# A fused attention and expert kernel on one core: queries' exponentials as weights, division with tokens on partitions

## The chip, the core and the metric

The kernel runs on one core of a Trainium2 chip. The metric is the device time of one execution in microseconds (us). Three runs of the kernel before took 1261.27 to 1263.55 us, median 1263.35 us.

## What is computed

Three parts follow each other. First a linear attention with 4 batches, 8 heads, 576 tokens and 64 features a head:

```python
def phi(x):
    proj = np.einsum('bhsd,df->bhsf', x, w_phi)
    proj = proj - np.max(np.abs(proj), axis=-1, keepdims=True)
    return np.concatenate([np.exp(proj), np.exp(-proj)], axis=-1)
q_p, k_p = (phi(q), phi(k))
kv = np.einsum('bhsf,bhsd->bhfd', k_p, v)
num = np.einsum('bhsf,bhfd->bhsd', q_p, kv)
den = np.einsum('bhsf,bhf->bhs', q_p, np.sum(k_p, axis=2))[..., None] + 1e-06
return num / den
```

Its output, 2304 tokens of width 512, goes through four experts, weighted by the rows' shares `p`: `out += p[:, e:e+1] * (relu(x @ w1[e]) @ w2[e])`, with an inner width of 1024. Last comes `((x @ v1) * (x @ v2) @ w3) @ w_out`. All data are fp32.

## The kernel before, in words

Two heads of one batch make a pair; there are 16 pairs, `p` from 0 to 15. For each pair, `k_side(p)` (L506) projects the keys (tile `P`, L540), takes each token's largest absolute value, subtracts it, forms the two exponentials (`E`, L525) and sums the products with the values, to which columns of ones are appended, into `kvp` (L553). Projections of the two heads stand on different halves of the rows of TensorE's array, the sums on different halves of its columns ("tiled" below). The result goes to `KV`.

`q_side(p, KV)` (L605) treats each head's 576 queries in two slices of 288 tokens, with the features on partitions. The host has written each q twice, and L613 and L614 make of the copies a rounded part and a remainder, stacked on 128 partitions. Two matmuls (L623, L624) project them, ScalarE copies the result (L628), GpSimd takes the largest absolute value over the partitions (L631), VectorE subtracts it (L634), and ScalarE forms the exponentials `Eq` (L639). The product with `KV` (L655) gives numerators on 64 partitions and the denominator, repeated, on the other 64. For pairs 6 to 15 (`SPLIT`), `KV` and `Eq` are split into rounded part and remainder (L594, L645, L647) and multiplied in three passes; for pairs 0 to 5 the product is in fp32. In the records an fp32 matmul counts as two instructions. ScalarE copies the product to `xq` (L660). One row of denominators a head is gathered by DMA to `d9` (L664), inverted (L667, L670), written to DRAM (L671) and read back to all partitions (L675); VectorE multiplies (L680) into the rows `xr`. These DMAs are all issued by SP. `plain_x` splits the first blocks of tokens for the experts.

The experts' work is a list of visits (L745). A visit holds a quarter of an expert's inner width and one or more blocks of 384 tokens (`pairs` there are pairs of blocks). In the plain form (`plain_up`, L806) a block has 24 up matmuls of 384 columns; in the Strassen form (`strassen_up`, L812) two blocks have 42. A block's `down` (L863) has three groups of six matmuls of 512 columns, each summed by VectorE (L890). The first `KA` = 8 quarters are plain for the first two blocks, so that they can run between the parts of attention; for the first `EB` = 5 of them each block has a visit of its own. When all attention is done, `phase_c` (L1053) closes the pools of attention, and the Strassen visits begin. The folds (L930) multiply `w3` and `w_out` into one matrix, two before each of the first `KA` visits of the second round.

No engine's order is written by hand. Every operation is given to `Prog` with an engine, an estimated time and a priority; `simulate` (L148) places it when its inputs are there and a buffer of its tile is free, `deadlines` (L254) gives the other engines due times from TensorE's order, and the order found is what is issued. Each engine then works in order. Up to `FILLED` (110 us of the planned time) `run` (L281) puts matmuls on zeros (`filler`, L472, tile `fill_z`) where the plan leaves TensorE idle. `AHEAD` (L62) says where in the visits the pairs from 4 on are due. PSUM has eight banks: in attention three for the visits (`mma`) and five for attention (`kv` 1, `kp` 2, `qp` 1, `num` 1).

## Time and profile before

| | before |
|---|---|
| median of 3 runs | 1263.35 us |
| the profiled execution | 1263.01 us |
| its span in the trace | 1261.2 us |
| TensorE busy | 1247.6 us, 99% |
| VectorE busy | 934.2 us, 74% |
| ScalarE busy | 628.4 us, 50% |
| GpSimd busy | 546.9 us, 43% |

In the rows PE is TensorE (PEld its weight loads), DVE VectorE, ACT ScalarE, POOL GpSimd, SP SyncE, which issues the DMAs. A timeline row is a run of equal instructions: start and length in us, engine, line, operation, output<-inputs, shapes, count, and in brackets idle time before it and what ended it. Matmuls overlap in the array, so a run's length includes the way through it; the next run's start shows when it has left the entrance free. The span is from the first to the last record; the profiled execution's own time has 1.8 us more.

### The profile page before, as it was taken

The page shows a single profiled execution, that of the slowest core. Times are in us where ns is not written, and L with a number is a line of the kernel's source. Part 1 is how long each engine was busy: PE and PEld are TensorE (multiplying, and loading weights), DVE is VectorE, ACT ScalarE, POOL GpSimd, SP SyncE. Part 2 cuts the span into 40 slices and gives each one's busy share as a digit, 9 for nine tenths or more (in the row PEclk, how much of TensorE's full clock was granted, in tenths as well). Part 3 has the DMA queues.
Part 4 walks back from the last instruction along what each step waited for, and adds up shares of the span by engine and source line. Part 5 has one row for each costly group of instructions (what it writes and reads, how often), then busy time and mean ns, then how long its engine had stood idle before and what let it go on. Part 6 is the DMA issues. An engine that isn't in the chain of part 4 may idle for free.

```text
span 1261.2 us, 19437 instructions
## 1 busy us (share of the span) xinstructions
PE 1247.6 (99%) x7449; PEld 1125.8 (89%) x7449; DVE 934.2 (74%) x1446; ACT 628.4 (50%) x1231; POOL 546.9 (43%) x374
## 2 busy tenths in 40 slices
PE   8999999999999999999999999999999999999998
PEld 7779988899999999988889888898899999999997
DVE  6698999979787885587687785698998647634454
ACT  7888888745433333344434343454445545443321
POOL 3432323316333333054544455466676677435220
PEclk9999999999999999999999999999999999999999
DMA  5654454222333321023535432143332212211002
GB/s 173 176 183 130 146 176 140 79 88 84 109 110 109 109 92 43 19 87 121 163 121 176 145 131 83 52 134 115 123 100 78 79 51 84 84 34 51 1 1 100
DMA packets 53197, 128.55 MB, mean 102 GB/s; under 512 B 10352, under 2 KB 14832, under 8 KB 53104
## 3 DMA queue, kind: packets, MB, share of 16 engines
q1 hardware_dynamic: 53104, 127.32, 31.5%
q8 instruction: 58, 0.95, 0.3%
q14 instruction: 35, 0.29, 0.1%
HBM read 109.84 MB, written 17.38 MB: 101 GB/s over the span
## 4 chain that ended last, share of the span: by engine, by line
PE 90%; DVE 5%; DMA 2%; ACT 2%; issue 1%; SPq 0%; DVEq 0%; ACTq 0%
PE dn L869 38%; PE upa L800 13%; PE upb L800 7%; PE up L800 4%; PE psw L940 3%; PE upc L800 3%; PE num L655 3%; PE kvp L553 1%; PE upa_4a L800 1%; PE upa_3b L800 1%; PE upa_3a L800 1%; PE upa_5b L800 1%; PE upa_5a L800 1%; PE upa_4b L800 1%; DVE xr L680 1%
## 5 line engine op out<-in xcount | busy, mean ns | idle before, releaser
L869 PE MATMUL dn<-w_b,h 128*128 128x512 f32 x1728 | 423.7, 391 | 0.0
L869 PEld LDWEIGHTS dn<-w_b,h 128*128 128x128 f32 x1728 | 320.7, 188 | 57.5 <-DVE acc L890 0.3
L391 POOL TENSOR_TENSOR w_a<-raw_a,w_a 128x768 fp32r<-128x768 f32 (+2 forms) x80 | 165.5, 2069 | 227.5 <-ACT w_a L389 202.1
L890 DVE SCALAR_TENSOR_TENSOR acc<-dn,pn,acc 128x512 f32<-128x512 f32 x270 | 200.3, 745 | 54.5 <-PE dn L869 52.6
L391 POOL TENSOR_TENSOR w_b<-raw_b,w_b 128x1024 fp32r<-128x1024 f32 x48 | 122.7, 2555 | 228.3 <-ACT w_b L389 223.2
L631 POOL PARTITION_ALL_REDUCE M<-Ps x64 | 86.4, 1361 | 169.5 <-ACT Ps L628 135.0
L800 PE MATMUL upa<-x_T,w_a 128*128 128x384 f32 x720 | 146.2, 337 | 0.0
L800 PEld LDWEIGHTS upa<-x_T,w_a 128*128 128x128 f32 x720 | 128.5, 187 | 7.2 <-ACT s L823 0.7
L823 ACT COPY s<-upa 128x384 f32<-128x384 f32 x120 | 57.5, 479 | 121.2 <-PE upa L800 120.9
L419 POOL TENSOR_TENSOR raw_a<-raw_a 128x256 f32<-128x256 f32 x128 | 109.8, 858 | 18.3 <-DVE acc L890 6.2
L389 ACT CAST w_b<-raw_b 128x1024 fp32r<-128x1024 f32 x61 | 64.3, 1054 | 103.4 <-PE dn L869 62.7
L869 PE MATMUL dn<-w_b,g 128*128 128x512 f32 x432 | 105.7, 390 | 0.0
L389 ACT CAST w_a<-raw_a 128x1024 fp32r<-128x1024 f32 (+2 forms) x93 | 84.5, 908 | 41.1 <-PE upb L800 16.6
L869 PEld LDWEIGHTS dn<-w_b,g 128*128 128x128 f32 x432 | 80.5, 188 | 13.7
L800 PE MATMUL up<-x_B,w_a 128*128 128x384 f32 x384 | 72.2, 338 | 0.0
L655 PE MATMUL num<-Eq,KV 128*128 128x288 f32 x336 | 67.4, 334 | 3.3 <-ACT xq L660 1.8
L800 PEld LDWEIGHTS up<-x_B,w_a 128*128 128x128 f32 x384 | 66.2, 188 | 1.0
L655 PEld LDWEIGHTS num<-Eq,KV 128*128 128x128 f32 x336 | 51.8, 188 | 10.9 <-ACT xq L660 3.8
L639 ACT ACTIVATE Eq<-Ps 128x288 f32<-128x288 f32 x128 | 51.5, 458 | 15.7 <-DVE Ps L634 15.4
L920 DVE TENSOR_TENSOR oacc<-dn,oacc 128x512 f32<-128x512 f32 x54 | 36.8, 687 | 19.0 <-PE dn L869 18.8
L800 PE MATMUL upa<-x_B,w_a 128*128 128x384 f32 x240 | 49.1, 339 | 0.0
L800 PE MATMUL upb<-x_B,w_a 128*128 128x384 f32 x240 | 49.0, 339 | 0.0
(213 smaller groups left out, 2241.7 us busy)
## 6 DMA issues: line engine op xcount, KB each, us to landing
raw_a<-w SPq DMA_DIRECT2D x37, 512.0 KB, 3.4
raw_b<-w SPq DMA_DIRECT2D x37, 512.0 KB, 3.7
qr<-qT SPq DMA_DIRECT2D x32, 288.0 KB, 3.2
near<-w3T SPq DMA_DIRECT2D x16, 512.0 KB, 4.2
raw_b<-near_wo SPq DMA_DIRECT2D x16, 512.0 KB, 4.3
near<-v SPq DMA_DIRECT2D x16, 512.0 KB, 4.8
vx<-vt SPq DMA_DIRECT2D x16, 330.0 KB, 4.3
kr<-kT SPq DMA_DIRECT2D x15, 320.0 KB, 3.9
```

What stands on the lines that cost most here:

```text
L389: lambda: op(ACT, act(n, sbuf), lambda: nc.scalar.copy(out=hi(), in_=raw[1]()), reads=[*raw[:1], *raw[2:]], fills=[w], after=after),
L391: lambda: op(eng, ns, lambda: e.tensor_tensor(out=lo(), in0=raw[1](), in1=hi().bitcast(F32), op=ALU.subtract), reads=[raw[0], w, *raw[2:]] ...
L419: ops.append(lambda to=to, a=a, b=b, how=how: op(POOL, gp(256), lambda: nc.gpsimd.tensor_tensor(out=raw()[:, to], in0=raw()[:, a], in1=raw ...
L631: op(POOL, 1300, lambda M=M, Ps=Ps: nc.gpsimd.partition_all_reduce(M(), Ps(), channels=128, reduce_op=bass_isa.ReduceOp.absmax), reads=[Ps ...
L639: op(ACT, act(HS), lambda a=a, E=E, Ps=Ps: nc.scalar.activation(out=E()[:, a], in_=Ps(), func=AF.Exp, scale=1.0 - 2 * a), reads=[Ps], fill ...
L655: nc.tensor.matmul(num(), KV[i]()[:, a, 2 * h:2 * h + 2].rearrange("p c d -> p (c d)"), EE[j]()[:, a], start=n == 0, stop=n == len(parts) - 1)
L800: nc.tensor.matmul(ps(), w()[:, a, i, kk * 128:kk * 128 + 128], x()[:, j, kk], start=first and n == 0, stop=last and n == total - 1, skip_ ...
L823: op(ACT, act(TB, False), lambda: nc.scalar.copy(out=t(), in_=ps()), reads=[ps], writes=[t], after=start["C"])
L869: nc.tensor.matmul(ps(), hs[fc]()[:, x, t * 128:(t + 1) * 128], w()[:, fc * 2:fc * 2 + 2, y], start=fc == 0 and n == 0, stop=fc == 1 and n ...
L890: op(DVE, dve(DM) + 61, lambda a=a, ps=ps, share=share: nc.vector.scalar_tensor_tensor(out=a(), in0=ps(), scalar=share(), in1=a(), op0=ALU ...
L920: op(DVE, dve(DM), lambda a=a, ps=ps: nc.vector.tensor_tensor(out=a(), in0=ps(), in1=a(), op=ALU.add), reads=[ps], writes=[a])
L940: nc.tensor.matmul(ps(), wa[v]()[:, k, a, f * 128:f * 128 + 128], wb[v]()[:, 2 * k:2 * k + 2, b], start=g == 0 and k == 0 and n == 0, stop ...
```

## The change

**Queries.** q comes once, with the two heads on the two halves of the partitions. A pair's 576 tokens are two chunks of 256 and 320; for pairs 0 to 3 a chunk of 384 comes first and the other 192 tokens after pair 3's first chunk (`BACK`). Rounded part and remainder of q are projected in three passes, each head on 64 rows of the array, the heads alternating; pair 0 in fp32. The exponentials are now the weights: 64 tokens at a time, on one half of the array's columns, with 66 columns of `KV` moving, in fp32 for every pair. Numerators and denominator come out with tokens on partitions; VectorE adds 1e-6, takes the reciprocal and multiplies, TensorE turns each tile of 128 tokens back (`turn`), and ScalarE copies it to `xr`. The splits of `KV` and of the exponentials, `xq`, the trip through DRAM and the last multiplication are gone. `KV` is one copy.

**Banks.** `mma` has two banks during attention, `qp` two; `num` has one, which from pair 3 on holds a chunk's products and then its turned tiles. After attention a third bank (`mmx`) is shared with `mma` by downs and turns that are not plain.

**Visits.** `KA` is 6 and `EB` 4; four folds come before the last two visits of the first Strassen round, the others two by two before the second round's. The first Strassen visit's weights are prepared by VectorE instead of GpSimd.

**Planner.** Its estimates for the tiled operations are new, each change between full, row-tiled and column-tiled operations is priced at 95 ns (`SWITCH`), and among operations that lie within `SAME` = 8 places in order one of the current mode is preferred. `AHEAD` is smaller.

The diff, without the lines that only hand the new arguments through and without the old `q_side`, which stands above:

```diff
@@ -36,19 +36,29 @@
-KA = 8
-EB = 5
-SPLIT = (6, 7, 8, 9, 10, 11, 12, 13, 14, 15)
+KA = 6
+EB = 4
+MORE = 3
+FIRST = 384
+BACK = (3, 3, 3, 3)
-ROWS = 220.0
-COLUMNS = 130.0
-ALONE = 3
+EXACT = (0,)
+QBUFS = 2
+EQ = 4
+KVS = 5
+ROWS = 111.0
+COLUMNS = 58.3
@@ -59,12 +69,12 @@
-AHEAD = (0.05, 0.6, 1.5, 2.4, 2.9, 4.5, 5.5, 6.5, 7.5, 8.5, 9.5, 10.5)
+AHEAD = (0.04, 0.43, 1.08, 1.73, 2.09, 3.24, 3.96, 4.68, 5.4, 6.12, 6.84, 7.56)
-NEAR = (24, 8, 0)
+NEAR = (40 - 2 * (16 - KA), 8, 0)
@@ -179,6 +194,9 @@
+            if o.eng == "PE" and o.mode != mode[0]:
+                o.end += self.SWITCH
+                mode[0] = o.mode
@@ -206,6 +224,13 @@
+            if same and e == "PE" and got is not None and got[2].mode != mode[0]:
+                near = [x for x in ready[e] if x[0] <= got[0] + same and x[2].mode == mode[0] and fits(x[2])]
+                if near:
+                    held.append(got)
+                    got = min(near)
+                    ready[e].remove(got)
+                    heapq.heapify(ready[e])
@@ -287,7 +312,7 @@
-            done = self.simulate(lambda o: place[o] if o.eng == "PE" else due[o])
+            done = self.simulate(lambda o: place[o] if o.eng == "PE" else due[o], self.SAME)
@@ -321,7 +346,7 @@
-    pools["mma"] = ec(tc.tile_pool(name="mma", bufs=3, space=PSUM))
+    pools["mma"] = ec(tc.tile_pool(name="mma", bufs=2, space=PSUM))
@@ -408,18 +433,18 @@
-    def strassen_tasks(src, nm, reads=(), after=()):
+    def strassen_tasks(src, nm, reads=(), after=(), eng=POOL):
+        e, ns = (nc.gpsimd, gp(256)) if eng == POOL else (nc.vector, dve(256))
@@ -481,9 +506,8 @@
-        op(DVE, 200, lambda: nc.vector.memset(wlo().bitcast(F32), 0.0), writes=[wlo])
-            out=wlo()[0:64], in0=wphi()[0:64], in1=wst()[0:64].bitcast(F32), op=ALU.subtract
+            out=wlo(), in0=wphi(), in1=wst().bitcast(F32), op=ALU.subtract
@@ -540,7 +564,7 @@
-            o = op(PE, nt * ROWS + 305, proj, reads=[kr, wphi], writes=P)
+            o = op(PE, (2 * nt + 1) * ROWS, proj, reads=[kr, wphi], writes=P, mode="rows")
@@ -555,7 +579,7 @@
-                op(PE, nt * 2 * COLUMNS + 250, total, reads=[E, w], writes=[kvp])
+                op(PE, (4 * nt + 1) * COLUMNS, total, reads=[E, w], writes=[kvp], mode="columns")
@@ -576,116 +600,103 @@
         for t0, nt in KG0 if not p else KG:
             group(t0, nt) if t0 < 4 else rest()
 
...
+        KV = V("at", [128, 2, 2, 66], F32, "KV", KVS, f"KV{p}")
+        op(ACT, act(264, False), lambda: nc.scalar.copy(out=KV(), in_=kvp()), reads=[kvp], writes=[KV])
+        return KV
+    def load_q(p, o, n):
+        b, pr = divmod(p, 4)
+        qr = V("at", [128, n], F32, "qr", 2, f"qr{p}_{o}")
+        dma(lambda: nc.sync.dma_start(out=qr(), in_=qT[b, pr][:, o:o + n]), n * 542, writes=[qr])
+        return qr
+    def q_side(p, KV, at=0, chunks=(256, 320)):
+        b, pr = divmod(p, 4)
+        width = sum(chunks)
+        qr = load_q(p, at, width) if p or at else qr0
+        rows = [slice(h * 64, h * 64 + 64) for h in range(2)]
+        if p in EXACT:
+            terms = [(lambda: wphi(), lambda: qr())]
+            used = [qr, wphi]
         else:
...
+            q2 = V("at", [128, 2, width], F32R, "q2", QBUFS, f"q2{p}_{at}")
+            op(ACT, act(width), lambda: nc.scalar.copy(out=q2()[:, 0], in_=qr()), reads=[qr], writes=[q2])
+            op(DVE, dve(width), lambda: nc.vector.tensor_tensor(
+                out=q2()[:, 1], in0=qr(), in1=q2()[:, 0].bitcast(F32), op=ALU.subtract
             ), reads=[qr], writes=[q2], port=True)
...
+            terms = [(lambda i=i: (wst, wlo)[i](), lambda j=j: q2()[:, j]) for i, j in PASSES]
+            used = [q2, wst, wlo]
+        for s, n in enumerate(chunks):
+            o0 = sum(chunks[:s])
+            sl = slice(o0, o0 + n)
+            nt = (n + 64) // 128
+            Pq = [V("aps", [128, n], F32, "qp", 2, f"Pq{p}_{h}{at}{s}") for h in range(2)]
+            def proj(Pq=Pq, sl=sl):
+                for x, (a, q) in enumerate(terms):
+                    for h in range(2):
+                        nc.tensor.matmul(Pq[h](), a()[rows[h]], q()[rows[h], sl], start=x == 0, stop=x == len(terms) - 1,
+                                         skip_group_check=True)
+            op(PE, n * 2.5 if len(terms) == 1 else 3 * mm(n), proj, reads=used, writes=Pq, mode="rows")
+            num = V("aps", [128, nt, 2, 66], F32, "num", 1, f"num{p}_{at}{s}")
+            for h, P in enumerate(Pq):
+                nm = f"{p}_{h}{at}{s}"
+                Ps = V("at", [128, n], F32, "Ps", 2, f"Ps{nm}")
+                op(ACT, act(n, False), lambda P=P, Ps=Ps: nc.scalar.copy(out=Ps(), in_=P()), reads=[P],
                    writes=[Ps])
...
+                M = V("at", [128, n], F32, "M", 2, f"M{nm}")
+                op(POOL, 250 + 3.65 * n, lambda M=M, Ps=Ps: nc.gpsimd.partition_all_reduce(
                     M(), Ps(), channels=128, reduce_op=bass_isa.ReduceOp.absmax
...
+                ), reads=[Ps], writes=[M], port=600 * n / HS)
+                op(DVE, dve(n), lambda M=M, Ps=Ps: nc.vector.tensor_tensor(
                     out=Ps(), in0=Ps(), in1=M(), op=ALU.subtract
                 ), reads=[M], writes=[Ps], port=True)
...
+                E = V("at", [128, 2, n], F32, "Eq", EQ, f"Eq{nm}")
                 for a in range(2):
...
+                    op(ACT, act(n), lambda a=a, E=E, Ps=Ps: nc.scalar.activation(
                         out=E()[:, a], in_=Ps(), func=AF.Exp, scale=1.0 - 2 * a
                     ), reads=[Ps], fills=[E])
...
+                def product(num=num, E=E, h=h, n=n, nt=nt):
+                    for t in range(nt):
+                        for a in range(2):
+                            for c in range(2):
+                                o = min(t * 128 + c * 64, n - 64)
+                                nc.tensor.matmul(
+                                    num()[c * 64:c * 64 + 64, t, h], E()[:, a, o:o + 64], KV()[:, a, h],
+                                    start=a == 0, stop=a == 1, skip_group_check=True,
+                                )
+                op(PE, (4 * nt + 1) * COLUMNS, product, reads=[KV, E], fills=[num], mode="columns")
+            d = V("at", [128, nt, 2], F32, "d", 2, f"d{p}_{at}{s}")
+            op(DVE, 100, lambda num=num, d=d: nc.vector.tensor_scalar(
+                out=d(), in0=num()[:, :, :, 64], scalar1=1e-6, scalar2=None, op0=ALU.add
+            ), reads=[num], writes=[d])
+            op(DVE, 110, lambda d=d: nc.vector.reciprocal(out=d(), in_=d()), writes=[d])
+            xt = V("at", [128, nt, 2, 64], F32, "xt", 2, f"xt{p}_{at}{s}")
+            op(DVE, dve(nt * 128), lambda num=num, d=d, xt=xt, nt=nt: nc.vector.tensor_tensor(
+                out=xt(), in0=num()[:, :, :, 0:64], in1=d().unsqueeze(3).to_broadcast([128, nt, 2, 64]), op=ALU.mult
+            ), reads=[num, d], writes=[xt])
+            T = V(*(("mma", [128, nt * 128], F32, "mm", 2) if p < MORE else ("aps", [128, nt * 128], F32, "num", 1)), f"T{p}_{at}{s}")
+            def turn(T=T, xt=xt, nt=nt):
+                for t in range(nt):
+                    nc.tensor.transpose(
+                        T()[:, t * 128:t * 128 + 128], xt()[:, t].rearrange("p h d -> p (h d)"), eye()
+                    )
+            op(PE, 110 * nt, turn, reads=[xt, eye], writes=[T])
+            for done, k, j, o in runs(b * S + at + o0, n):
+                op(ACT, act(k, False), lambda T=T, done=done, k=k, j=j, o=o: nc.scalar.copy(
+                    out=xraw(j)()[:, pr, o:o + k], in_=T()[:, done:done + k]
+                ), reads=[T], fills=[xraw(j)])
+            if b < 2 and not at and not s:
+                plain_x(b, pr)
 
     raws = {}
 

@@ -744,10 +755,14 @@
-    visits += [("expert", c, (1, 0), None) for c in range(KA, NE * NQ)]
+    folds = deque(("fold", n, (), None) for n in range(16))
+    for c in range(KA, NE * NQ):
+        if c >= NE * NQ - (8 - KA):
+            visits += [folds.popleft(), folds.popleft()]
+        visits.append(("expert", c, (1, 0), None))
-        if c < KA:
-            visits += [("fold", 2 * c, (), None), ("fold", 2 * c + 1, (), None)]
+        if folds:
+            visits += [folds.popleft(), folds.popleft()]
@@ -761,15 +776,15 @@
-    def prefetch(v, after=()):
+    def prefetch(v, after=(), eng=POOL):
-            made.append(split_tasks(src1, "ring1", f"a{v}", after=after) if kind == "plain" else strassen_tasks(src1, f"a{v}"))
-            made.append(split_tasks(src2, "ring2", f"b{v}", after=after, eng=DVE if kind == "plain" else POOL))
+            made.append(split_tasks(src1, "ring1", f"a{v}", after=after) if kind == "plain" else strassen_tasks(src1, f"a{v}", eng=eng))
+            made.append(split_tasks(src2, "ring2", f"b{v}", after=after, eng=DVE if kind == "plain" else eng))
@@ -788,8 +803,13 @@
-    def bank(width, name, pool="mma"):
-        return V(pool, [128, width], F32, "mm", 3 if pool == "mma" else 5, name)
+    banks = [0]
+    def bank(width, name, pool="mma", late=False):
+        if late:
+            banks[0] += 1
+            pool = ("mma", "mma", "mmx")[banks[0] % 3]
+        return V(pool, [128, width], F32, "mm", {"mma": 2, "mmx": 1, "mmb": 5}[pool], name)
@@ -861,7 +881,7 @@
-        ps = bank(DM, f"dn{nm}")
+        ps = bank(DM, f"dn{nm}", late=visits[int(nm.split("_")[0])][0] != "plain")
@@ -894,7 +914,7 @@
-                ps = bank(TB, f"tr{i}_{t}{d}")
+                ps = bank(TB, f"tr{i}_{t}{d}", late=True)
@@ -967,7 +987,7 @@
-                    prefetch(v + 1)
+                    prefetch(v + 1, eng=DVE)
@@ -1047,13 +1067,14 @@
-    qr0 = load_q(0, 0)
+    qr0 = load_q(0, 0, FIRST)
+        open_pool("mmx", bufs=1, space=PSUM)
@@ -1064,13 +1085,17 @@
+    sides = {}
-        KV = k_side(p)
+        sides[p] = k_side(p)
-        q_side(p, KV)
+        q_side(p, sides[p], 0, (FIRST,) if p < 4 else (256, 320))
+        for back in range(4):
+            if BACK[back] == p:
+                q_side(back, sides[back], FIRST, (S - FIRST,))
@@ -1110,9 +1135,7 @@
-        "qT": np.repeat(lay(q, (B, 4, 2, 1, S, D), (0, 1, 2, 3, 5, 4), (B, 4, 2, 1, D, S)), 2, 3).reshape(
-            B, 4, 2, 2 * D, S
-        ),
+        "qT": lay(q, (B, 4, 2, S, D), (0, 1, 2, 4, 3), (B, 4, 2 * D, S)),
```

## Rows read from the trace of the kernel before

**Rows 1.** the page's busy times, TensorE's line.

```profile
PE 1247.6 (99%) x7449; PEld 1125.8 (89%) x7449; DVE 934.2 (74%) x1446; ACT 628.4 (50%) x1231; POOL 546.9 (43%) x374
```

**Rows 2.** windows of 50 us: stretch, length, busy time (instructions), TensorE's clock, DMA share.

```profile
0.00:50.00 50.00, 45.56 (x503) 36.72 (x504) 33.33 (x68) 37.35 (x102) 19.21 (x21) 1.00 0.54 160
50.00:100.00 50.00, 47.44 (x454) 39.96 (x452) 41.62 (x79) 44.25 (x109) 18.15 (x13) 1.00 0.63 193
...
200.00:250.00 50.00, 48.05 (x431) 43.18 (x431) 46.66 (x83) 40.41 (x96) 16.87 (x13) 1.00 0.33 101
```

**Rows 3.** groups by form, TensorE: the filler.

```profile
L474 PE MATMUL kvp<-fill_z 128*128 128x248 bf16 x113 | 15.6, 285 | 2.3 <-DVE fill_z L470 1.0 <-ACT KV L586 0.9 <-ACT KV L591 0.3
```

**Rows 4.** TensorE's timeline at the start: start, length (us), line, tiles, instructions.

```profile
24.51 1.16 PE L540 MATMUL P<-wphi,kr 64*128 64x128 f32 x16
...
50.14 2.08 PE L474 MATMUL kvp<-fill_z 128*128 128x248 bf16 x18
52.08 0.49 PE L562 MATMUL P_r<-wphi,kr 128*128 128x128 f32 x2
...
84.66 2.33 PE L800 MATMUL up<-x_B,w_a 128*128 128x384 f32 x12
```

**Rows 5.** TensorE's waits from 85 to 300 us: total, times, longest.

```profile
PE num L655 <- ACT xq L660: 1.5, 3, 0.7
PE num L655 <- DVE KV L594: 1.4, 2, 0.9
```

**Rows 6.** TensorE's timeline: tiled runs, full groups and transposes.

```profile
12.09 0.69 PE L553 MATMUL kvp<-vx,E 128*64 128x66 f32 x16
12.71 1.16 PE L540 MATMUL P<-wphi,kr 64*128 64x128 f32 x16
...
19.03 1.15 PE L553 MATMUL kvp<-vx,E 128*64 128x66 f32 x32
20.11 2.21 PE L655 MATMUL num<-Eq,KV 128*128 128x288 f32 x8
22.25 1.15 PE L553 MATMUL kvp<-vx,E 128*64 128x66 f32 x32
...
149.82 1.16 PE L540 MATMUL P<-wphi,kr 64*128 64x128 f32 x16
150.91 2.37 PE L800 MATMUL up<-x_B,w_a 128*128 128x384 f32 x12
153.12 0.96 PE L655 MATMUL num<-Eq,KV 128*128 128x288 f32 x6
153.92 0.30 PE L623 MATMUL Pq<-q,wst 128*128 128x288 f32 x1
...
154.18 2.25 PE L800 MATMUL up<-x_B,w_a 128*128 128x384 f32 x12
156.27 0.96 PE L655 MATMUL num<-Eq,KV 128*128 128x288 f32 x6
...
563.36 1.14 PE L901 MATMUL tr<-eye,acc 128*128 128x128 f32 x9
564.26 1.30 PE L800 MATMUL upa<-x_B,w_a 128*128 128x384 f32 x6
```

**Rows 7.** groups by form, VectorE: mean of one in ns.

```profile
L890 DVE SCALAR_TENSOR_TENSOR acc<-dn,pn,acc 128x512 f32<-128x512 f32 x270 | 200.3, 745 | 54.5 <-PE dn L869 52.6
...
L647 DVE TENSOR_TENSOR Eq<-Eq,Eq 128x576 fp32r<-128x576 f32 x40 | 30.9, 773 | 1.4 <-ACT Eq L645 1.3
```

**Rows 8.** the page's costliest groups: down matmuls and all-reduces.

```profile
L869 PE MATMUL dn<-w_b,h 128*128 128x512 f32 x1728 | 423.7, 391 | 0.0
...
L631 POOL PARTITION_ALL_REDUCE M<-Ps x64 | 86.4, 1361 | 169.5 <-ACT Ps L628 135.0
```

**Rows 9.** TensorE's timeline where attention ends and the Strassen form begins.

```profile
267.12 0.95 PE L655 MATMUL num<-Eq,KV 128*128 128x288 f32 x6
...
294.92 1.20 PE L800 MATMUL upa<-x_B,w_a 128*128 128x384 f32 x6
```

More of the change, by code (lines that the diff above doesn't have):

```diff
@@ L119 @@
     COLD = 4500.0
+    SWITCH = 95.0
+    SAME = 8
     OTHER = {"DVE": "POOL", "POOL": "DVE"}
@@ L146, in op, with simulate @@
         return o
-    def simulate(self, key):
+    def simulate(self, key, same=0):
         for o in self.ops:
@@ L530, in group @@
         def group(t0, nt):
-            where = ("mma", "mm", 3) if not p and t0 == 2 else ("aps", "kp", 2)
+            where = ("mma", "mm", 2) if not p and t0 == 2 else ("aps", "kp", 2)
             P = [V(where[0], [128, nt, FEAT], F32, *where[1:], f"P{p}_{t0}{h}") for h in range(2)]
@@ L577, in k_side @@
             group(t0, nt) if t0 < 4 else rest()
-        halves = [
-            (lambda t: t()[:, :, 0:4:3], lambda: kvp()[:, :, :, 0:64]),
-            (lambda t: t()[:, :, 1:3], lambda: kvp()[:, :, :, 64:65].to_broadcast([128, 2, 2, 64])),
-        ]
-        if p not in SPLIT:
-            KV = [V("at", [128, 2, 4, 64], F32, "KV0", 2, f"KV{p}")]
-            for part, src in halves:
-                op(ACT, act(256, False), lambda part=part, src=src: nc.scalar.copy(out=part(KV[0]), in_=src()),
-                   reads=[kvp], fills=KV)
-        else:
-            KV = [V("at", [128, 2, 4, 64], F32R, f"KV{i}", 2 - i, f"KV{i}_{p}") for i in range(2)]
-            for part, src in halves:
-                op(ACT, act(256, False), lambda part=part, src=src: nc.scalar.copy(out=part(KV[0]), in_=src()),
-                   reads=[kvp], fills=KV[:1])
-            for part, src in halves:
-                op(DVE, dve(256), lambda part=part, src=src: nc.vector.tensor_tensor(
-                    out=part(KV[1]), in0=src(), in1=part(KV[0]).bitcast(F32), op=ALU.subtract
-                ), reads=[kvp, KV[0]], fills=KV[1:])
@@ L650, in q_side @@
-                num = V(*(("mma", [128, HS], F32, "mm", 3) if p < ALONE else ("aps", [128, HS], F32, "num", 1)), f"num{nm}")
-                parts = [(a, i, j) for a in range(2) for i, j in (PASSES if len(EE) == 2 else PASSES[:1])]
-                def product(num=num, parts=parts, EE=EE, h=h):
-                    for n, (a, i, j) in enumerate(parts):
-                        nc.tensor.matmul(
-                            num(), KV[i]()[:, a, 2 * h:2 * h + 2].rearrange("p c d -> p (c d)"), EE[j]()[:, a], start=n == 0, stop=n == len(parts) - 1
-                        )
@@ L659, in q_side @@
-                op(PE, len(parts) * (mm(HS) if len(EE) == 2 else mm4(HS)), product, reads=KV + EE, writes=[num])
-                op(ACT, act(HS, False), lambda num=num, h=h, sl=sl: nc.scalar.copy(
-                    out=xq()[:, h, sl], in_=num()
-                ), reads=[num], fills=[xq])
-            dr = 64 - 64 * h
-            dma(lambda h=h, dr=dr: nc.sync.dma_start(
-                out=d9()[h * 64:(h + 1) * 64], in_=xq()[dr:dr + 1, h].rearrange("o (p c) -> o p c", p=64)
-            ), 2304, reads=[xq], fills=[d9])
@@ L678, in q_side @@
-        for done, n, j, o in runs(b * S, S):
-            for h in range(2):
-                op(DVE, dve(n) + 105, lambda h=h, done=done, n=n, j=j, o=o: nc.vector.tensor_tensor(
-                    out=xraw(j)()[h * 64:h * 64 + 64, pr, o:o + n], in0=xq()[h * 64:h * 64 + 64, h, done:done + n],
-                    in1=r()[h * 64:h * 64 + 64, done:done + n], op=ALU.mult,
-                ), reads=[xq, r], fills=[xraw(j)], port=True)
-        if b < 2:
-            plain_x(b, pr)
+                def product(num=num, E=E, h=h, n=n, nt=nt):
[7 more added lines that the diff above has]
+                                )
```

70 lines of the change are left out of this document (10 added, 60 removed).

## The prediction

> **What bounds the kernel now.** I read the page first: TensorE is busy for 1247.6 of 1261.2 us [rows 1], and its granted clock is the full one (2.4 GHz) in every window read [rows 2]. So time can come from two places only: TensorE work that is no longer needed, and stretches in which TensorE does nothing useful. The windows say where the second kind is: the first 100 us hold 4.4 + 2.6 = 7.0 us without TensorE work, a later window 1.95 us [rows 2]. But "busy" there includes filler: 113 matmuls on zeros [rows 3], put in where the planner expects a gap. Eighteen of them took 52.08 - 50.14 = 1.94 us [rows 4], so all are about 113 x 0.108 = 12.2 us. Until the first expert matmul at 84.66 us [rows 4], then, TensorE idles 7.0 + 12.2 = 19.2 us. After that the waits of TensorE sum to 2.9 us [rows 5]; the experts' plain visits fill every hole. From there on the kernel is as long as its matmuls, and ScalarE, VectorE and GpSimd count only if they make TensorE wait. VectorE is close to that: 46.66 of 50 us between 200 and 250 us [rows 2].
>
> Because matmuls are pipelined, their cost is read from the timeline as the distance of the starts, not as busy time.
>
> **The change part by part.** *Query products.* A slice of 288 tokens of one head is now six matmuls, start to start 153.92 - 153.12 = 0.80 us, or for pairs 0 to 5 two fp32 ones of two records each, 2.14 us for two slices [rows 6]. There are 40 and 24 such slices: 40 x 0.80 + 24 x 1.07 = 57.7 us.
>
> The new products (exponentials as weights, 66 columns moving, two column halves) have exactly the shape of the keys' sums: 16 records take 12.71 - 12.09 = 0.62 us, 32 take 20.11 - 19.03 = 1.08 us [rows 6]. So 16 more cost 0.46 us, 0.0288 us a record, and 0.16 us is paid at the beginning. A pair needs 5 token tiles x 2 heads x 4 matmuls x 2 records = 80 records, 2.30 us, for 16 pairs 36.8 us.
>
> *Query projections.* Now two matmuls a slice, 0.26 us (153.92 to 154.18) up to some 0.45 us where the previous group is short; at 0.36 us, my middle, 64 slices are 23 us. Afterwards six matmuls a chunk on 64 rows, the two heads side by side. The nearest row is the keys' projection: 16 records, 1.09 us (149.82 to 150.91) [rows 6]; less the 0.16 us entry this is 0.93 us for 8 side-by-side pairs of 256 column cycles, 0.454 ns a column. Three passes over 576 tokens: 3 x 576 x 0.454 = 0.785 us a pair, 12.6 us in all. If the heads did not overlap it would be 25.2 us.
>
> *Turning.* Five transposes a pair; nine took 564.26 - 563.36 = 0.90 us [rows 6], so 80 x 0.10 = 8.0 us, all new.
>
> *Changes of mode.* Entering a tiled run costs the 0.16 us above; leaving one costs the next full group 2.21 instead of 2.09 us for 12 matmuls (150.91 to 153.12 against 154.18 to 156.27) [rows 6], 0.12 us. So a tiled run among full matmuls costs 0.28 us beyond its records. A pair adds six: two projections, four products. Each alone: 6 x 0.28 x 16 = 26.9 us; where the two heads' products, or a projection and the keys' one, stand together, three runs remain, 13.4 us. The changed planner prices a switch and prefers a ready operation of the same mode; I take four, 17.9 us.
>
> The page "TensorEngine Tiling (Array Packing)" of the Trainium skill (Key Properties) says that changing the tiling mode drains TensorE. The 0.16 and 0.12 us agree with a drain at each change; by this rule with nothing grouped the six-run sum would hold, which is the second rival below.
>
> Sum on TensorE: 57.7 + 23 = 80.7 us becomes 36.8 + 12.6 + 8.0 + 17.9 = 75.3 us, **-5.4 us**; bounds -9.9 us (three runs) and +16.2 us (six runs, and no overlap of heads).
>
> *Two quarter experts fewer in plain form.* KA from 8 to 6: a plain visit of two blocks has 48 up matmuls, the other form 42. Twelve matmuls take 2.09 us, so 2 x 6 x 0.174 = **-2.1 us**.
>
> *The start.* The first block needs 384 tokens of four pairs. Now those pairs run all 576 tokens, and the denominators travel through DRAM: a gather, a write and two broadcasts on SP's queue, then two multiplications a run of tokens. Afterwards only 384 tokens come first, nothing leaves the chip, and the split, the copy of numerators and half of the casts are gone from ScalarE and VectorE. The keys of pair 1 start at 12.71 us [rows 6], those of pair 2 at 24.51 us [rows 4], 11.8 us apart; I put this at 8 for two thirds of the query work, so four pairs and a tail end near 45 us. TensorE's useful work by then is 4 x 4 us of keys (1.09 + 2 x 1.08 us and two small groups, an estimate), 4 x 3.1 us of queries (two thirds of 75.3 / 16) and the 4 us of pair 4's keys, 32 us, so about 12 of 45 us are idle. Against 19.2 us: **-7 us**; bounds 0 (the pairs run no faster) and -13 us (only the first 6 us stay idle).
>
> *Fewer plain visits as cover.* Twelve plain block turns instead of sixteen remain to fill holes during attention. What they must cover shrinks: VectorE loses the 40 splits of exponentials, 30.9 us [rows 7], the stacked split of q, the keys' low parts and the multiplications by 1/denominator, and gains per chunk two small operations and one division out of PSUM. At no more than the same 773 ns for each division, 32 of them are 25 us, without the small ones. So VectorE is not made the bound, and I cost this at nothing; if the cover fails, see the first rival.
>
> *Two banks instead of three* for the plain visits. A down group is six matmuls of 423.7 / 1728 = 0.245 us [rows 8], 1.47 us; its sum on VectorE takes 0.745 us [rows 7]. With two banks the third group waits unless the first was emptied within one group's time, so anything over 0.7 us ahead of that sum on VectorE stalls TensorE, and every matmul is queued behind it. In mixed stretches attention stands between; in the plain stretch at the end of attention it does not. About 9 groups x 0 to 1 us; I take **+3 us** with the other new waits, bounds 0 and +9.
>
> *At nothing:* the fold groups moved forward (same matmuls, now between experts), three weight loads fewer, half the q traffic, and the first Strassen weights on VectorE instead of GpSimd. TensorE's other work covers all four; uncovered, the last would show as one wait of a few us at the first Strassen matmul.
>
> Sum: -5.4 - 2.1 - 7 + 3 = -11.5 us. The profiled execution took 1263.01 us with a span of 1261.2 us; 1263.0 - 11.5 = **1251.5 us**. It lies 0.3 us below the median of the runs, 1263.35 us, which changes nothing.
>
> **Rivals.** *Slower: the single num bank.* From pair 3 on a chunk's numerators and its turned tile share one PSUM bank: both heads' products, the addition, the reciprocal, the division, the turn and ScalarE's copy come one after another, and the next chunk's products, on TensorE in order with everything behind them, wait for that. My estimate of the chain is 1.5 us of products (48 records on average), 1.8 us for three VectorE operations of 0.3 to 0.77 us [rows 7] and 1.2 us for turn and copy, 4.5 us when nothing is in the way; if the second head's exponentials come only behind its own all-reduce (1.36 us [rows 8]), about 6 us. Pairs 4 to 15 have 24 chunks. In the trace attention's last products start at 267.12 us and the first Strassen matmul at 294.92 us [rows 9], 28 us later. Four block turns (24 up and 18 down matmuls, 8.6 us each) and 11.5 us fewer put that matmul near 249 us, so attention must end by 221 us: (221 - 45) / 24 = 7.3 us a chunk is the point from which it decides. At 8 us a chunk TensorE stands 24 x 0.7 = 17 us, 1268 us; at 9 us 41 us, 1292 us. For it: VectorE's load; against it: exponentials get four buffers, so they run ahead. 0.13.
>
> *Nothing gained: the mode changes eat it.* Each run alone (+3.6 instead of -5.4) and a start that gives only 1 us: 1263.0 + 3.6 - 2.1 - 1 + 3 = 1266.5; with one of both, about 1259 to 1262. For it: in the trace tiled groups mostly stand alone [rows 6]; against it: the four products of a pair become ready two by two. 0.10.
>
> *More gained.* Three runs a pair, no bank wait and the start at -13: 1263.0 - 9.9 - 2.1 - 13 = 1238; with the keys' own runs merged too, 1234. For it: the filler and the idle time are both of the start, and a start bound by chains shrinks with the chain. 0.20.
>
> **How the numbers follow.** My case has 0.57 with a range of its own of 1244 to 1260. The range of all reaches to 1236 below and to 1267 above, which leaves out most of the bank case and the outermost part of the largest gain. A measurement of this kernel can tell about 0.2%, 2.5 us, from no change, so faster means below 1260.8 and slower above 1265.9. Faster: my case, the larger gain and a little of the third, 0.79. Same: 0.08, from the mode changes. Slower: 0.13.
>
> **What would show it.** Right: the first expert matmul near 45 us; filler well under 113; 80 product records a pair at about 29 ns inside a run; TensorE waits of a few us after the start. Wrong: waits of products or turns for ScalarE's copy or VectorE's division summing to more than 10 us (the bank); projections of the two heads one behind the other; a plain down matmul waiting for VectorE's sum by more than 10 us in all; TensorE without work before the first Strassen product.

## The result and the profile after

The changed kernel takes 1243.37 us (median; 1242.25 to 1243.83), the kernel before, run beside it, 1262.31 us: ratio 0.9849, 95% interval 0.9832 to 0.9866, 18.9 us less. The profiled execution's span is 1240.5 us against 1261.2.

The page's busy times of the changed kernel, the line that answers to [rows 1]:

```profile
PE 1233.4 (99%) x8504; PEld 1114.2 (90%) x8504; DVE 875.3 (71%) x1394; ACT 584.7 (47%) x1143; POOL 549.3 (44%) x381
```

Windows of 50 us as in [rows 2]; TensorE's busy time stands first, VectorE's third:

```profile
0.00:50.00 50.00, 47.31 (x785) 39.34 (x787) 35.71 (x82) 38.93 (x99) 19.55 (x20) 1.00 0.60 187
50.00:100.00 50.00, 50.00 (x785) 45.45 (x780) 37.45 (x82) 39.20 (x104) 20.24 (x16) 1.00 0.43 140
100.00:150.00 50.00, 50.00 (x722) 44.05 (x720) 40.04 (x82) 36.42 (x92) 17.44 (x14) 1.00 0.39 114
150.00:200.00 50.00, 50.00 (x769) 44.32 (x769) 37.78 (x77) 37.12 (x96) 17.18 (x14) 1.00 0.30 93
200.00:250.00 50.00, 49.34 (x475) 43.91 (x470) 34.30 (x59) 24.09 (x50) 10.40 (x8) 1.00 0.12 38
```

TensorE has work everywhere but in the first window and for 0.7 us near the end of attention. VectorE, at 46.7 of 50 us between 200 and 250 us before, is at 34.3 there and at 35.7 to 40.0 in the other windows shown. The filler, the products and the turns by form, as in [rows 3]:

```profile
L670 PE MATMUL num<-KV,Eq 128*64 128x66 f32 x1280 | 44.1, 224 | 0.0
...
L499 PE MATMUL kvp<-fill_z 128*128 128x248 bf16 x96 | 14.5, 288 | 2.7 <-ACT KV L604 1.7 <-DVE warm L506 1.0
L689 PE MATMUL T<-eye,xt 128*128 128x128 f32 x80 | 14.3, 277 | 0.0
```

Adding up the distances of starts over TensorE's whole timeline gives where the time went (a distance counts up to the end of its matmul; what lies beyond is idle):

| us | before | after |
|---|---|---|
| query products | 57.5 | 40.3 |
| query projections | 23.4 | 18.6 |
| turns of the queries | 0 | 9.7 |
| the keys' matmuls | 64.8 | 63.5 |
| up matmuls, all forms | 541.6 | 540.9 |
| down matmuls | 495.5 | 496.9 |
| folds and turns of expert sums | 50.9 | 50.9 |
| filler | 14.0 | 12.6 |
| idle | 9.9 | 3.4 |
| behind the last matmul | 3.7 | 3.7 |
| span (sum, rounded) | 1261.2 | 1240.5 |

Of 20.7 us between these two executions, 13.6 are matmuls of attention and 7.9 are filler and idle time; the experts' matmuls take 0.7 us more. In the middle of attention TensorE's timeline now reads (start, length, as in [rows 6]):

```profile
93.17 0.50 PE L642 MATMUL Pq<-q,wst 64*128 64x256 f32 x4
93.51 0.28 PE L642 MATMUL Pq<-q,wlo 64*128 64x256 f32 x2
93.72 1.15 PE L577 MATMUL kvp<-vx,E 128*64 128x66 f32 x32
94.70 1.57 PE L670 MATMUL num<-KV,Eq 128*64 128x66 f32 x48
96.10 1.10 PE L577 MATMUL kvp<-vx,E 128*64 128x66 f32 x32
97.13 0.49 PE L586 MATMUL P_r<-wphi,kr 128*128 128x128 f32 x2
```

The products of both heads are one run of 48 records (1.40 us) and stand between two of the keys' runs: all 112 records are entered and left once. Over the whole kernel a run of one tiled mode (its records have 64 rows or 64 columns) comes 50 times before, always with records of the keys, and 79 times after. Where attention ends, as in [rows 9]:

```profile
234.16 1.62 PE L670 MATMUL num<-KV,Eq 128*64 128x66 f32 x48
...
238.59 0.49 PE L689 MATMUL T<-eye,xt 128*128 128x128 f32 x3
...
244.50 1.20 PE L820 MATMUL upa<-x_B,w_a 128*128 128x384 f32 x6
...
246.52 1.15 PE L820 MATMUL upb<-x_T,w_a 128*128 128x384 f32 x5 [0.66 <-DVE x_T L416]
```

The last products start at 234.16 us, the first Strassen matmul at 244.50 us, 10 us later; before it was 28.

### The profile page after: what moved, and what is told of

The parts are those of the page before. It is cut to its first block, busy times and chain, and to the rows that moved or that the text cites. A ratio compares the mean times of both kernels' runs of the same rounds, so it can differ in the third digit from the quotient of the medians.

```text
span 1240.5 us, 21285 instructions
## 1 busy us (share of the span) xinstructions
PE 1233.4 (99%) x8504; PEld 1114.2 (90%) x8504; DVE 875.3 (71%) x1394; ACT 584.7 (47%) x1143; POOL 549.3 (44%) x381
## 4 chain that ended last, share of the span: by engine, by line
PE 97%; DVE 1%; ACT 1%; DMA 1%; SPq 0%; issue 0%; DVEq 0%; ACTq 0%
PE dn L889 40%; PE upa L820 14%; PE upb L820 7%; PE up L820 4%; PE upc L820 4%; PE psw L960 4%; PE num L670 3%; PE kvp L577 2%; PE upa_4a L820 1%; PE upa_3b L820 1%; PE upa_3a L820 1%; PE upa_5b L820 1%; PE upa_5a L820 1%; PE upa_4b L820 1%; PE Pq L642 1%; PE P L564 1%
## 5 line engine op out<-in xcount | busy, mean ns | idle before, releaser
L820 PE MATMUL upa<-x_T,w_a 128*128 128x384 f32 x756 | 153.2, 337 | 0.0
L820 PEld LDWEIGHTS upa<-x_T,w_a 128*128 128x128 f32 x756 | 135.0, 187 | 7.0
L653 POOL PARTITION_ALL_REDUCE M<-Ps x64 | 81.3, 1312 | 132.0 <-ACT Ps L650 112.2
L414 ACT CAST w_a<-raw_a 128x768 fp32r<-128x768 f32 (+2 forms) x94 | 84.6, 900 | 54.6 <-PE upb L820 22.5
L661 ACT ACTIVATE Eq<-Ps 128x256 f32<-128x256 f32 (+3 forms) x128 | 47.6, 436 | 19.2 <-PE num L670 16.5
L820 PE MATMUL up<-x_B,w_a 128*128 128x384 f32 x288 | 54.8, 341 | 0.0
L820 PE MATMUL upb<-x_T,w_a 128*128 128x384 f32 x252 | 51.1, 336 | 0.7 <-DVE x_T L416 0.7
L656 DVE TENSOR_TENSOR Ps<-Ps,M 128x256 f32<-128x256 f32 (+3 forms) x64 | 38.0, 596 | 18.1 <-POOL M L653 18.1
L820 PE MATMUL upc<-x_B,w_a 128*128 128x384 f32 x252 | 50.8, 336 | 0.0
L820 PEld LDWEIGHTS up<-x_B,w_a 128*128 128x128 f32 x288 | 49.6, 188 | 1.0 <-DVE d L680 0.2
```

Source lines behind the costliest of these rows:

```text
L414: lambda: op(ACT, act(n, sbuf), lambda: nc.scalar.copy(out=hi(), in_=raw[1]()), reads=[*raw[:1], *raw[2:]], fills=[w], after=after),
L653: op(POOL, 250 + 3.65 * n, lambda M=M, Ps=Ps: nc.gpsimd.partition_all_reduce(M(), Ps(), channels=128, reduce_op=bass_isa.ReduceOp.absmax), ...
L656: op(DVE, dve(n), lambda M=M, Ps=Ps: nc.vector.tensor_tensor(out=Ps(), in0=Ps(), in1=M(), op=ALU.subtract), reads=[M], writes=[Ps], port=True)
L661: op(ACT, act(n), lambda a=a, E=E, Ps=Ps: nc.scalar.activation(out=E()[:, a], in_=Ps(), func=AF.Exp, scale=1.0 - 2 * a), reads=[Ps], fills ...
L820: nc.tensor.matmul(ps(), w()[:, a, i, kk * 128:kk * 128 + 128], x()[:, j, kk], start=first and n == 0, stop=last and n == total - 1, skip_ ...
```

## The experiments

Three theories stood at the beginning. M: most of the gain is TensorE work in attention. S: it is the earlier start. V: it is the relief of VectorE, which lets plain turns go. All times are medians; the kernel before took 1262.1 to 1262.9 us beside them.

**Planner blind to modes.**

```diff
-    SWITCH = 95.0
-    SAME = 8
+    SWITCH = 0.0
+    SAME = 0
```

> The changed kernel, but its planner neither prices a change of tiling mode (0 instead of 95 ns) nor prefers an operation of the current mode (SAME 0 instead of 8). Theory M (most of the gain is TensorE work in attention, and it came out larger than forecast because tiled runs stand together): the tiled runs fall apart, at 0.28 us for each one more; with one to three more runs a pair that is 4 to 13 us over the changed kernel's 1243.4 us, 1247 to 1256 us. Theory S (the gain is the earlier start) and theory V (the gain is the relief of VectorE): within 2 us of 1243.4 us.

Measured 1249.5 us, ratio 0.9899 (0.9884 to 0.9914): 6.1 us over the changed kernel, inside M's range. By the sums of starts products, projections, turns and keys' runs are 5.3 us longer together, up matmuls 0.9 and idle time 1.3; the matmuls are the same. Tiled runs rise from 79 to 99: 20 more at the forecast's 0.28 us are 5.6 us, an estimate that fits. S and V had no place for this.

**Every product twice.**

```diff
-                    for t in range(nt):
+                    for t in [*range(nt), *range(nt)]:
```

> The changed kernel with every query product done twice into the same place (the result is the same), so 1280 more records of the products' shape. Theory M (attention is bound by TensorE's entrance, every record costs its distance of starts): 1280 x 0.029 us = 37 us more, 1278 to 1284 us. Theory V (attention is bound by VectorE or another engine and TensorE has room): less than 15 us more, under 1258 us.

Measured 1276.3 us, ratio 1.0111 (1.0094 to 1.0128), 32.9 us more; the products' sum rose from 40.3 to 77.0 us, 28.6 ns for each added record, and 3.1 us of filler gave way. Added records cost nearly their full distance of starts, so TensorE's entrance bounds attention; the time is 1.7 us under M's range, which had left out the filler.

**Heads one behind the other.**

```diff
-                for x, (a, q) in enumerate(terms):
-                    for h in range(2):
+                for h in range(2):
+                    for x, (a, q) in enumerate(terms):
```

> The changed kernel with the projections of a chunk's two heads one behind the other instead of alternating. If the two halves of the array's rows work side by side only for neighbours, the three passes of each head go serially: 12.6 us of records become about 25 us, 10 to 14 us more, 1253 to 1257 us. If they never worked side by side, or if projections are hidden: within 2 us of 1243.4 us.

Measured 1242.3 us, ratio 0.9843 (0.9829 to 0.9858): no change, and the expectation of 10 us was a miss. The reading "never side by side" is not the reason, though. TensorE's timeline of this run, then of the changed kernel:

```profile
156.06 0.57 PE L642 MATMUL Pq<-q,wst 64*128 64x320 f32 x4
156.46 0.32 PE L642 MATMUL Pq<-q,wlo 64*128 64x320 f32 x2
156.71 1.15 PE L577 MATMUL kvp<-vx,E 128*64 128x66 f32 x32
```

```profile
156.89 0.56 PE L642 MATMUL Pq<-q,wst 64*128 64x320 f32 x4
157.29 0.31 PE L642 MATMUL Pq<-q,wlo 64*128 64x320 f32 x2
157.53 1.15 PE L577 MATMUL kvp<-vx,E 128*64 128x66 f32 x32
```

Six matmuls of 320 columns take 0.65 and 0.64 us with the change of mode; one behind the other, at the 0.174 us that an up matmul of 384 columns takes, they would need 6 x 320 / 384 x 0.174 = 0.87 us without it (an estimate). They overlap in both, and with the heads apart the records still begin with four of `wst` and end with two of `wlo`, though the program has `wst`, `wst`, `wlo` of one head first. So the second head's stream had begun before the first one's last pass: here the two halves ran independently of each other.

**Whole queries at the start.**

```diff
-FIRST = 384
+FIRST = 576
-        q_side(p, sides[p], 0, (FIRST,) if p < 4 else (256, 320))
+        q_side(p, sides[p], 0, (256, 320))
```

(the loop over `BACK` then does nothing, and `plain_x` of batch 0 follows the second chunk)

> The changed kernel without the early first chunk: pairs 0 to 3 run all 576 queries in two chunks, as the later pairs do, and the first block is split for the experts after the second chunk. Theory S (the gain is the earlier start): the start gives back most of the gain, 8 to 15 us over 1243.4 us, 1251 to 1258 us, with the first expert matmul near 75 us. Theory M (most of the gain is TensorE work in attention): the matmuls stay the same and only filler and idle time at the start grow: 0 to 4 us, at most 1247 us.

Measured 1240.9 us, ratio 0.9825 (0.9810 to 0.9839). Without the early chunk it is no slower, 2.5 us faster by the medians, with intervals that just overlap. So the early chunk is not where the gain comes from. The first up matmul comes at 60.5 us in both, 24 us earlier than before: this run does not undo the earlier start itself. What the start gives stays within the 7.9 us of filler and idle time in the table, so S cannot be most of the gain.

**The old attention with the new list of visits, the new attention with the old list.**

```diff
 # kernel before
-KA = 8
-EB = 5
+KA = 6
+EB = 4
```

(the folds move forward and `NEAR` becomes 20, as in the change; these lines are left out)

> The kernel before with the changed kernel's list of visits alone (KA 6, EB 4, four folds moved forward), its attention as it was. Theory V (the relief of VectorE is what lets four plain turns go): attention, with VectorE nearly full, ends late and TensorE runs out of plain work; four turns are 33 us, VectorE's part of them some 20 us, so TensorE idles 8 to 20 us: 1268 to 1282 us. Theory M (cover was never short): only the twelve-matmul saving of each quarter shows, 2.1 us less, 1259 to 1261 us.

```diff
 # changed kernel
-KA = 6
-EB = 4
+KA = 8
+EB = 5
```

(the first Strassen weights stay with VectorE)

> The changed kernel with the list of visits of before (KA 8, EB 5), so four plain turns more during attention. Theory M: 2 x 12 up matmuls more of 0.174 us, 2.1 us plus the ends of runs: 1245 to 1248 us. If the changed kernel were short of cover: no slower, 1240 to 1243.4 us. Theory V (VectorE decides attention): VectorE gets 20 us more to do, 5 us or more, over 1248 us.

The first took 1285.9 us, ratio 1.0176 (1.0161 to 1.0192): 23 us more than before, above V's range. The second took 1250.3 us, ratio 0.9901 (0.9887 to 0.9916): 6.9 us more than the changed kernel. So at the old list the rest of the change (new attention, planner, early weights) gives 12.7 us; the new list adds 7 us in the new kernel and costs 23 us in the old one. In the second, by the sums of starts, up matmuls account for 2.4 us, down matmuls for 1.8 and idle time for 3.2; the largest wait of its TensorE (total, times, longest) is this, behind the last turns of the plain stretch:

```profile
PE dn L889 <- DVE h L877: 3.2, 4, 1.2
```

In the first, TensorE's waits and timeline show where it stands:

```profile
PE upb L804 <- ACT w_a L389: 8.6, 1, 8.6
PE upa L804 <- ACT x_B L389: 4.9, 1, 4.9
...
PE upb L804 <- POOL w_a L391: 1.6, 1, 1.6
```

```profile
269.18 0.96 PE L655 MATMUL num<-Eq,KV 128*128 128x288 f32 x6
...
280.53 0.69 PE L804 MATMUL upa<-x_B,w_a 128*128 128x384 f32 x1 [4.94 <-ACT x_B L389]
...
293.09 1.01 PE L804 MATMUL upb<-x_T,w_a 128*128 128x384 f32 x2 [8.64 <-ACT w_a L389]
295.73 1.65 PE L804 MATMUL upb<-x_T,w_a 128*128 128x384 f32 x4 [1.63 <-POOL w_a L391]
297.18 2.12 PE L804 MATMUL upc<-x_B,w_a 128*128 128x384 f32 x6
299.10 1.29 PE L804 MATMUL upa<-x_T,w_a 128*128 128x384 f32 x6
300.23 1.23 PE L804 MATMUL upa<-x_B,w_a 128*128 128x384 f32 x6
301.30 1.20 PE L804 MATMUL upa<-x_T,w_a 128*128 128x384 f32 x6
```

Attention's last products come 2.1 us later than before (269.18 against 267.12 us). The rest of the loss lies behind them: the first Strassen visit waits for the split tokens until 282 us and for its own weights until 293 to 296 us. And the stop costs more than itself: the six matmuls from 297.18 us take 1.92 us, six of the same shape from 300.23 us 1.07 us. In the window from 250 to 300 us the mean granted clock is 0.80, part of it at the lower level (1.2 GHz), after TensorE had stood:

```profile
250.00:300.00 50.00, 33.53 (x214) 28.99 (x214) 39.66 (x49) 22.80 (x44) 23.80 (x15) 0.80 0.10 29
```

**The planner alone.** The kernel before with the new estimates, `mode`, `SWITCH` and `SAME` (an excerpt):

```diff
+                o.end += self.SWITCH
+                mode[0] = o.mode
-            done = self.simulate(lambda o: place[o] if o.eng == "PE" else due[o])
+            done = self.simulate(lambda o: place[o] if o.eng == "PE" else due[o], self.SAME)
```

> The kernel before with the changed planner alone: the new estimates for the keys' tiled operations, the price of a mode change and the preference for the current mode; no operation is changed. Theory M: attention's matmuls stay, only the keys' runs can stand together: 0 to 3 us less than before, 1259 to 1262 us. If the planner were the main gain: 8 us or more, under 1254 us.

Measured 1274.0 us, ratio 1.0094 (1.0077 to 1.0111): slower, which no theory had. The keys' runs did not merge (50 tiled runs in both, 64.6 against 64.8 us), and attention's last product came at 279 us instead of 268; idle time rose by 6 us, most of it again the first Strassen visit's wait for weights. By itself this planner is no gain; why it orders the old attention worse stays open.

**Is it VectorE's load?**

```diff
 # kernel before with KA 6, EB 4
-SPLIT = (6, 7, 8, 9, 10, 11, 12, 13, 14, 15)
+SPLIT = ()
```

> The kernel before with the changed list of visits (as in the run that took 1285.9 us) and no pair split: products of all 16 pairs in fp32, so VectorE loses 30.9 + 7.5 us of subtractions and ScalarE 27.8 us of casts, while TensorE gets 40 x (1.07 - 0.80) = 11 us more to do. Theory V (VectorE's load sets the end of attention, and so how many plain turns can go): the idle time before the Strassen visits shrinks by more than TensorE gains: 1262.5 - 2.1 + 11 = 1271 us, 1266 to 1276 us. If chains of waits or TensorE itself set the end of attention: 1285.9 + 11 = 1297 us.

```diff
 # changed kernel, behind the exponentials
+                if p >= 6:
+                    X = V("at", [128, 2, n], F32, "X", 1, f"X{nm}")
+                    op(DVE, dve(2 * n), lambda E=E, X=X: nc.vector.tensor_tensor(
+                        out=X(), in0=E(), in1=E(), op=ALU.subtract
+                    ), reads=[E], writes=[X], port=True)
```

> The changed kernel with 40 idle subtractions of the old splits' size on VectorE (pairs 6 to 15, one for each head and chunk, result unused), some 31 us between 75 and 250 us, where VectorE is now busy 37 to 40 of each 50 us; nothing waits for them but a buffer of their own. Theory V: VectorE gets to 95% there, attention ends later than the plain turns can cover, and TensorE waits: 3 to 12 us over 1243.4 us, 1246 to 1256 us. If VectorE's relief was not needed: at most 2 us, under 1245.5 us.

The first took 1287.4 us, ratio 1.0200 (1.0185 to 1.0216): 38 us less for VectorE brought attention's end forward by only 1.8 us (last products at 267.40 against 269.18 us), and the same 8.64 us wait for weights remains. The 11 us more for TensorE, on which both expectations counted, did not come: the products took 57.8 us against 57.6 (sums of starts). So both forecasts were missed, and V's, which without those 11 us would have been still lower, more clearly. The second took 1244.9 us, ratio 0.9865 (0.9850 to 0.9880), 1.5 us more, although between 100 and 200 us VectorE is about as full as it was before (46.7 and 47.2 of 50 us; from 200 to 250 us it stays below, at 38.3 against 46.7):

```profile
100.00:150.00 50.00, 50.00 (x731) 43.77 (x730) 47.40 (x92) 34.64 (x89) 19.10 (x15) 1.00 0.37 114
150.00:200.00 50.00, 50.00 (x754) 43.56 (x754) 43.64 (x89) 36.96 (x94) 20.78 (x16) 1.00 0.29 94
```

V has fallen from both sides. So the 23 us need another cause, and the waits above name one.

**Theory W: the first Strassen weights.** In the diff, `strassen_tasks` on VectorE drops the wait for attention's end (`late` is empty). VectorE's timeline of the changed kernel shows its two splits before the last products at 234 us:

```profile
225.30 0.96 DVE L416 TENSOR_TENSOR w_a<-raw_a,w_a 128x768 fp32r<-128x768 f32 x1 [1.87 <-ACT w_a L414]
...
231.42 1.22 DVE L416 TENSOR_TENSOR w_a<-raw_a,w_a 128x1024 fp32r<-128x1024 f32 x1 [0.74 <-ACT w_a L414]
```

```diff
 # changed kernel
-                    prefetch(v + 1, eng=DVE)
+                    prefetch(v + 1)
```

> The changed kernel with one part undone: the first Strassen visit's weights are again prepared by GpSimd after attention's end, and not by VectorE before it. Theory W (what makes four plain turns dispensable is that the first Strassen weights are ready when attention closes): attention's last turn is at 239 us; with GpSimd the weights of the run with 1285.9 us were complete some 24 us after attention's end, of which the plain work left covers 5 to 10 us; TensorE stands 12 to 20 us: 1255 to 1265 us. Theory V (VectorE's relief in attention makes them dispensable, whoever prepares the weights): within 2 us of 1243.4 us.

Measured 1258.4 us, ratio 0.9971 (0.9959 to 0.9984): 15.0 us slower, in W's range; V has no place for it. Engine and time of the preparation move together here; which of the two counts was not tried apart. GpSimd's timeline of this run and TensorE's largest wait:

```profile
242.86 1.85 POOL L416 TENSOR_TENSOR w_a<-raw_a,w_a 128x768 fp32r<-128x768 f32 x1 [26.92 <-ACT w_a L414]
...
266.68 2.33 POOL L416 TENSOR_TENSOR w_a<-raw_a,w_a 128x1024 fp32r<-128x1024 f32 x1
```

```profile
PE upb L820 <- POOL w_a L416: 8.3, 1, 8.3
```

```diff
 # kernel before with KA 6, EB 4, and strassen_tasks as changed
-                    prefetch(v + 1)
+                    prefetch(v + 1, eng=DVE)
```

> The kernel before with the changed list of visits (as in the run that took 1285.9 us), and the first Strassen weights prepared by VectorE as soon as they are there. Theory W: most of the 18 us for which TensorE stood before the Strassen visits goes: 1264 to 1272 us. Theory V (the old attention ends too late for twelve plain turns): no less than 1280 us.

Measured 1278.3 us, ratio 1.0129 (1.0114 to 1.0144): 7.7 us won back, not the 14 to 22 expected; above W's range, below V's. The wait for weights is gone, and what remains is what comes behind the last products. TensorE's and VectorE's timelines:

```profile
265.58 0.95 PE L656 MATMUL num<-Eq,KV 128*128 128x288 f32 x6
...
276.15 0.69 PE L805 MATMUL upa<-x_B,w_a 128*128 128x384 f32 x1 [4.14 <-ACT x_B L389]
...
281.49 1.97 PE L805 MATMUL upb<-x_T,w_a 128*128 128x384 f32 x5 [0.77 <-DVE x_T L391]
```

```profile
269.04 0.22 DVE L671 RECIPROCAL d<-d 128x9 f32<-128x9 f32 x1
...
273.65 1.53 DVE L681 TENSOR_TENSOR xr<-xq,rb 64x576 f32<-64x576 f32 x2 [0.85 <-DMA rb<-rd]
275.22 0.96 DVE L730 TENSOR_TENSOR xr<-xr 128x768 f32<-128x768 f32 x1
```

The last pair's denominators are inverted at 269.04 us and are back from DRAM for the multiplication at 273.65 us; only then begin the differences for the Strassen form, and no plain turn is left beside them. The new attention has no such trip, and its order keeps 18 down and 24 up matmuls for behind the last products. How the rest divides between these two was not tried, nor the early weights with the old attention and its own list.

**One quarter fewer still** (`KA = 5`, whole queries at the start):

> The changed kernel with the whole queries at the start (as in the run that took 1240.9 us) and one quarter fewer in plain form, KA 5. Theory V with TensorE as the bound: 1 us of matmuls less, but two plain turns, 17 us of cover, go too; attention's last product came at 234 us and the first Strassen matmul at 244 us, so 6 us of cover are missing and TensorE waits: 1244 to 1249 us. If cover was still ample: 1239 to 1240.5 us.

Measured 1256.9 us, ratio 0.9956 (0.9939 to 0.9972), 16 us over the run with `KA` 6, where 3 to 8 were expected. The waits of its Strassen matmuls for the splits and differences of x begin at 236 us, for example:

```profile
PE upb L820 <- DVE x_T L416: 3.3, 2, 1.7
PE upa L820 <- ACT s L843: 2.0, 2, 1.5
```

Idle time is 9 us more than at `KA` 6, and up matmuls take 6 us longer, with a mean granted clock of 0.90 between 200 and 250 us and 0.93 in the next 50 us; the expectation had left the clock out. The cover is used up at `KA` 6. The best kernel run is the one with whole queries at the start, 1240.9 us.

Taken together: two thirds of the 20.7 us are TensorE work in attention, which is M. That the first Strassen weights are early is a condition of the rest: without it 15 of the 18.9 us are lost.

## Why the prediction was right, point by point

Forecast 1251.5 us, measured 1243.4 us: inside the range of 1236 to 1267 and just below that of my own case, 1244 to 1260. The gain was 18.9 us instead of 11.5 to 12.

- **Records of the products: right.** 36.8 us were forecast from the keys' shape; a doubled product costs 28.6 ns a record.
- **Changes of mode: mis-sized.** I took four runs a pair at the full price, 17.9 us. The four runs are there: 32 runs hold products and 32 hold projections. But 34 of these 64 also hold records of the keys (20 with their sums, 14 with their projections), so tiled runs rise only from 50 to 79, and 29 more at 0.28 us are 8.1 us, an estimate. Measured beyond the bare records are 40.3 - 36.8 = 3.5 us for products and 18.6 - 12.6 = 6.0 us for projections, 9.5 us together. So the attention term was not -5.4 but -12.2 us (80.8 to 68.6), and the keys gave 1.3 us more. That is 8.1 of the 9.2 us by which the two profiled executions (20.7 us apart) exceed the forecast's 11.5. By the page "TensorEngine Tiling (Array Packing)" of the Trainium skill (Key Properties) a change of mode drains TensorE, a change of tile alone does not; the run of 1.40 us between two of the keys' runs, 29 ns a record with no entry left, agrees. The planner's part of it is 6 us (blind: 1249.5 us).
- **Projections side by side: right**, by the rate, not by the order in which they are issued.
- **Turns: nearly right**, 9.7 for 8.0 us.
- **Quarters in Strassen form: right in its matmuls only**, 2.4 us of up matmuls between `KA` 8 and 6 where 2.1 were forecast; in the runs it is 6.9 us, since down matmuls and waits of the longer plain stretch come to it. Against the kernel before, up matmuls fell by 0.7 us and down matmuls rose by 1.4: 18 instead of 9 of them come right behind a tiled run, some 0.11 us longer each, so part of the price of a change of mode stands here.
- **Start and idle time: too small, and the picture wrong.** Forecast -7 us at the start and +3 for new waits, -4 together; filler and idle time fell by 7.9 us, since the +3 did not come. That this error and the one of the visits nearly cancel (3.9 us more, 2.8 us less) is luck. And the first expert matmul is at 60.5, not 45 us:

```profile
10.60 1.05 PE L564 MATMUL P<-wphi,kr 64*128 64x128 f32 x16
...
21.14 1.47 PE L564 MATMUL P<-wphi,kr 64*128 64x128 f32 x16
...
29.94 1.16 PE L564 MATMUL P<-wphi,kr 64*128 64x128 f32 x16
...
60.47 4.41 PE L820 MATMUL up<-x_B,w_a 128*128 128x384 f32 x24
```

  The keys of successive pairs stand 10.5 and 8.8 us apart; from 30 to 60 us TensorE does the other 192 tokens of pairs 0 to 3 and attention of pairs 4 to 6. The early first chunk gave nothing.
- **Two banks: no wait in the changed kernel.** TensorE waits for 3.4 us in all:

```profile
PE kvp L499 <- ACT KV L604: 1.7, 2, 1.2
PE kvp L499 <- DVE warm L506: 1.0, 1, 1.0
PE upb L820 <- DVE x_T L416: 0.7, 1, 0.7
```

  Those +3 us did not come; 3.2 us of waits in the plain stretch stand in the run with `KA` 8, there for VectorE's half of `h`, not for a bank. The wait that was meant, of a down matmul for VectorE's sum, shows in the run with late weights, 2.4 us in the plain stretch behind attention.
- **VectorE not made the bound: right**, shown by the idle load between 100 and 200 us.
- **"At nothing: the first Strassen weights on VectorE": wrong.** I named a wait of a few us if its cover were gone; undone, it costs 15 us: with late weights the four plain turns cannot be spared. For the same reason the 28 us between attention and the Strassen form, taken from [rows 9], were no fixed need: with early weights and fewer plain turns 10 us suffice. Attention's last products come at 234 us, 13 us behind the 221 us that the bank rival had worked out from the 28, and TensorE does not stand. Whether late weights alone made it 28 before is not shown: with early weights and `KA` 8 there are 38 us, filled with plain turns.
- **The rivals.** No wait for the num bank shows. Mode changes did not eat the gain. The third, more gained, came nearest: it named 1234 to 1238 us, from merged runs, no wait for a bank and 13 us at the start. Many runs are shared and the bank wait stayed away, but filler and idle time fell by 7.9 us, not 13.

## What to carry to other kernels

Price a tiled matmul by its records and by its runs: count which runs the plan will place side by side before charging each an entry and an exit. When work that covers a wait is taken away, ask what the next phase still has to prepare behind the barrier; moving that ahead of it (15 us here) can be what pays for the removal. Test a phase change in pairs: the list of visits was worth -7 us with one attention and +23 us with the other.

## What was not expected of the hardware

Two matmul streams on different halves of the array's rows run side by side even when the program issues one whole stream first: 0.65 us for six matmuls of 320 columns, against 0.64 us when they alternate. And a stop of TensorE goes on costing: in the 50 us that hold 16.5 us of idle time behind the old attention (the run of 1285.9 us) the mean granted clock was 0.80; from 250 to 300 us in the runs of 1258.4 and 1278.3 us, with shorter stops, it was 0.90.
